# A spectral mix and a 32-head attention on one core: exponentials' buffers given out from a list of free ones

## The chip, the cores and the metric

The kernel runs on one core of one Trainium2 chip. The core has five engines that run side by side, each with an instruction queue of its own: TensorE (PE, matmuls; PEld is its weight loads), VectorE (DVE), ScalarE (ACT), GpSimd (POOL) and SyncE (SP), which here issues all DMAs. Engines wait for each other by semaphores: an instruction can wait until a counter of another engine, or of its own, has reached a value. The metric is the device time of one execution in microseconds (us), lower is better.

## The reference

Two branches work on the same x of 2048 tokens by 640 features and are mixed by a gate for each token. Branch A is a Fourier mix over tokens and features, of which the real part is kept. Branch B is attention with 32 heads of 20 features, one key and one value head for all of them.

```python
a = x @ Wd_re.T;  b = x @ Wd_im.T                  # 640 x 640, along the features
yA = Ws_re @ a - Ws_im @ b                         # 2048 x 2048, along the tokens
q = (x @ wq) as 32 heads of 20;  k = x @ wk;  v = x @ wv
p = softmax(q @ k.T * 20 ** -0.5)                  # per head, 2048 x 2048
yB = concat(p @ v) @ wo
g = sigmoid((x * gate_w).sum(-1))
out = g * yA + (1 - g) * yB
```

## The kernel before

The first part projects q, k and v and forms a and b of branch A. The long middle part, of which the change is a part, runs both branches interleaved. The last part multiplies by wo and mixes.

The middle part runs over 16 pairs of heads; p is the pair, hh the head in it. For each pair there are 16 rounds: two halves qh of the queries, and eight steps kk, each of two blocks of 128 keys. A round issues by a table, a string of words:

- **b** (`b_unit`, from line 728): one matmul of scores for 128 keys and 512 queries into a PSUM bank, then one exponential on ScalarE from that bank to an SBUF buffer `pt` of 128x512. Eight a round. The exponentials of a round are numbered 0 to 7 here, in the order of the table.
- **V** (`av_step`, from line 745): the four matmuls that multiply four `pt` buffers by the values, which appear as eight in the trace (a burst of av). Two a round, and they work on the round before, which waits in the list `old`.
- **a** (`a_half`): a matmul of scores for the next pair and a VectorE reduction for its row maxima. Eight a round while pairs are left.
- **y** (`halves.run`): matmuls of branch A, in two row groups of the array; y0 uses rows 0 to 63, y1 rows 64 to 127, beside a and b of the other head in the other row group.
- **E**: moving a finished block of branch A out of PSUM on ScalarE.

The words carry the row group and the PSUM bank: `b1S3` is scores of head 1 in bank S3. Three of five rounds use `ROUND_10`, with 20 y, and then two use `ROUND_9`, with 18; the last pair uses `ROUND_LAST`, in which there are 48 y and no a. The order on PE, ACT, DVE and POOL is the order of the code, and the framework adds the semaphore waits. Banks are few, so a b reuses a bank that an earlier exponential of the same round has read: in every half of a round, the last b of one row group goes to the bank of exponential 0 (first half) or 4 (second half), and its weight load waits for that exponential.

The `pt` buffers come from a pool of 16 under one name (line 524), so that the pool gives them out in turn: an exponential takes the buffer of the exponential 16 before it. Before it may write, three things must have happened: its own scores are there, the av matmul that read the old content is done, and the exponential that wrote the old content is done. The first two are counts of PE, the third is a count of ACT itself. An ACT instruction carries one wait; for a second the framework puts a separate wait instruction, EVENT_SEMAPHORE, ahead of it in the queue, unless it can tell that one wait implies the other. In the built program ScalarE has 1211 of these, and 937 of them belong to line 739, the exponentials.

Of the kernel before, what the change touches and what calls it, by code (L numbers as in the profile page):

```python
# [8 lines left out]
F32 = mybir.dt.float32  # L9
# [8 lines left out]
P = 128  # L18
# [5 lines left out]
NT = S // P  # L24
# [5 lines left out]
ROW = 512  # L30
# [3 lines left out]
def kernel(  # L34
# [24 lines left out]
    def bank(tag, name):  # L59
        if tag in BANKS:  # L60
            turn[tag] += 1
            tag = BANKS[tag][(turn[tag] - 1) % len(BANKS[tag])]
        return psum.tile([P, ROW], F32, tag=tag, name=name, bufs=1)
# [290 lines left out]
    def tick():  # L354
        clock["n"] += 1
        due = [t for t in todo if t[0] <= clock["n"]]
        todo[:] = [t for t in todo if t[0] > clock["n"]]
        for _, f, args in due:
            f(*args)
# [4 lines left out]
    def a_half(hh, tag="A", main=False):  # L364
        u = state[hh]
        if u >= NA:
            return
        ins = a_unit(u, hh, tag)
        if main:
            halves.scored(ins)  # L370
        state[hh] = u + 1
        if state[1 - hh] <= u:
            return
        if u % 64 == 16 and u // 64 + 1 < NPAIR:
            load_qs(u // 64 + 1)
        if u % 64 == 63:
            later(1, a_reduce, u // 64)
            later(3, a_final, u // 64)
# [142 lines left out]
    cp = ctx.enter_context(tc.tile_pool(name="cp", bufs=1))  # L521
    cpools += [cp, cp]
    xp = ctx.enter_context(tc.tile_pool(name="xp", bufs=1))
    pp = ctx.enter_context(tc.tile_pool(name="pp", bufs=16))
    op = ctx.enter_context(tc.tile_pool(name="op", bufs=2))


# [118 lines left out]
    def y_evict():  # L646

        if not ended:
            return
        grp = ended[0]  # L650
        ps = grp["ps"]
        if "t" not in grp:
            grp["t"] = [op.tile([P, HALF], F32, name=("yt", "yu")[k]) for k in range(len(ps))]
            grp["left"] = list(range(len(ps)))
        k = grp["left"].pop(0)
        nc.scalar.activation(grp["t"][k], ps[k], AF.Copy)  # L656
        if not grp["left"]:
            ended.pop(0)
            y_out(grp)
# [65 lines left out]
    av = {}  # L725
    pt = {}

    def b_unit(p, hh, kc, qc, tag="B"):
        b = 64 * hh
        ps = bank(tag, f"b_{p}_{kc}_{qc}_{hh}")  # L730
        nc.tensor.matmul(  # L731
            ps,
            ks[b : b + 62, kc * P : (kc + 1) * P],
            qs[p][b : b + 62, qc * ROW : (qc + 1) * ROW],
            start=True,
            stop=True,
        )
        t = pp.tile([P, ROW], F32, name="pt")
        halves.scored(nc.scalar.activation(t, ps, AF.Exp, scale=SCALE))  # L739
        pt[(hh, kc, qc)] = t  # L740

    def av_mm(ps, g, t, kc, first, last):
        nc.tensor.matmul(ps[32 * g : 32 * g + 32, :], vsb[:, kc, :], t, start=first, stop=last)  # L743

    def av_step(p, qh, kc):
        if kc == 0:
            av[qh] = bank("V", f"av_{p}_{qh}")
        for hh in range(2):
            for j in range(2):
                av_mm(av[qh], 2 * hh + j, pt.pop((hh, kc, 2 * qh + j)), kc, kc == 0, kc == NT - 1)  # L750

    def finish_half(p, qh):
        ob = op.tile([P, ROW], F32, name="ob")
        nc.scalar.activation(ob, av[qh], AF.Copy)
        for hh in range(2):
            h = 2 * p + hh
            for j in range(2):
                js = slice((2 * qh + j) * ROW, (2 * qh + j + 1) * ROW)
                g = 32 * (2 * hh + j)
                move(sum_d[h : h + 1, js], ob[g + DH : g + DH + 1])  # L760
                move(oT_d[h * DH : (h + 1) * DH, js], ob[g : g + DH])
        if p == LAST:
            sm = op.tile([P, 16], F32, name="sm")
            ts = slice(qh * S // 2, (qh + 1) * S // 2)
            for hh in range(2):
                move(sm[64 * hh : 64 * hh + 64], sum_d[2 * p + hh, ts].rearrange("(s t) -> s t", t=16))
            later(4, finish_last, ts, sm)
        elif qh == 1:
            sm = op.tile([P, 32], F32, name="sm")
            move(sm, sum_d[2 * p : 2 * p + 2].rearrange("h (s t) -> (h s) t", t=32))  # L770
            later(24, finish_sums, p, sm)
# [11 lines left out]
    def finish_last(ts, sm):  # L783
# [9 lines left out]

    ROUND_10 = (
        "a1S0 y0 b1S3 y0 y0 b1S1 y0 y0 a1S2 y0 a1S5 y0 y0 a1S4 y0 b1S0 b0S3 V a0S1 y1 y1 b0S0 "
        "y1 y1 a0S5 y1 a0S3 y1 y1 b0S2 y1 y1 a0S4 y1 b0S0 b1S1 V y0"
    ).split()
    ROUND_9 = (  # L800
        "a1S2 y0 b1S0 y0 y0 a1S1 y0 a1S5 y0 y0 a1S4 y0 y0 b1S3 y0 b0S2 b1S0 V a0S5 y1 b0S2 y1 "
        "y1 a0S1 y1 b0S0 y1 y1 a0S3 y1 y1 a0S4 y1 E0 b1S2 b0S5 V"
    ).split()

    ROUND_LAST = (
# [3 lines left out]
    ).split()  # L809
    ROUNDS = [(p, qh, kk) for p in range(NPAIR) for qh in range(2) for kk in range(NT // 2)]  # L810

# [7 lines left out]
    for rnd in ROUNDS:  # L819
        p, qh, kk = rnd  # L820
        nb, na = [0, 0], 0
        turn = (p * NT + qh * SJ + kk) % 5
        new = [(p, qh, 2 * kk), (p, qh, 2 * kk + 1)]
        for what in ROUND_LAST if p == LAST else ROUND_10 if turn < 3 else ROUND_9:
            if what == "V":
                if old:
                    st = old.pop(0)
                    av_step(*st)
                    if st[2] == NT - 1:
                        finish_half(*st[:2])  # L830
                continue
            g = int(what[1])
            if what[0] == "y":
                halves.run(g)
            elif what[0] == "E":
                if p == LAST or turn == 4:
                    y_evict()
            elif what[0] == "b":
                b_unit(p, g, 2 * kk + nb[g] // 2, 2 * qh + nb[g] % 2, what[2:])
                if p == LAST and sum(nb) % 2 == 0:  # L840
                    tick()
                nb[g] += 1
            else:
                if na % 2 == 0:
                    tick()
                a_half(g, what[2:], True)
                na += 1
        old += new
        if p == LAST and qh == 1:
            for f in BEFORE.get(kk, ()):  # L850
                f()
# [7 lines left out]
    for i in range(2 * NT):  # L859
        tb, e = divmod(i, 2)  # L860
        if e == 0:
            gate_y(tb + 1)
        o_group(tb, e)
        tick()
        if i == 0:
            for st in old:
                av_step(*st)
            finish_half(*old[-1][:2])
        n, k = divmod(i, 4)
        if k == 1:  # L870
            mult_o(n + 2)
        elif k == 2:
            split_o(n + 2)
            load_o(n + 3 if n else NO)
        if e == 1:
            load_y(tb + 4)
# [47 lines left out]
```

## Time and profile before

| what | value |
|---|---|
| median of 3 runs | 1837.29 us |
| the three runs | 1836.1, 1837.29 and 9650.36 us |
| the profiled execution's own time | 1837.41 us |
| its span, first to last instruction | 1835.6 us |
| granted TensorE clock | 1.0 throughout |
| exponentials (line 739) | 2048, mean 598 ns |

The profile is one execution, recorded by the hardware. The page gives each engine's busy time and its share of the span, the chain of work that ended last, and groups of instructions by source line. A group's row reads: line, engine, operation, output<-input, shapes, count, busy time and mean time of one, and then the engine's idle time ahead of these instructions with what ended it. In the timeline a row is: start, length, engine, line, operation, names, count of merged instructions, and the idle time before with its releaser. Ends of matmuls are modelled. Times of the timeline are rounded to 0.01 us.

The middle part runs from about 260 us to 1590 us in the ordinary rounds and to about 1765 us in the last pair's.

### The profile page before, as it was taken

To read this page: it belongs to the slowest core of one execution; us is meant where nothing else is said; L and a number is where in the kernel's file an instruction comes from. 1 tells how busy PE (TensorE), PEld (TensorE's weight loads), DVE (VectorE), ACT (ScalarE), POOL (GpSimd) and SP (SyncE) were. 2 spreads that over 40 slices of the span, in tenths; PEclk is the share of its full clock that TensorE was granted. 3 is DMA by queue.
4 is the path that set the end of the run, shared out by engine and by line. 5 is a ranking of instruction groups with operands and counts; after the bars stand their busy time and mean duration, and the time that the engine had idled before them with its cause. 6 is when DMAs were issued, how large, how long until landed. Compare 5 with 4: busy or idle time off the path is not lost.

```text
span 1835.6 us, 41674 instructions
## 1 busy us (share of the span) xinstructions
PE 1819.7 (99%) x16344; PEld 1231.3 (67%) x16344; DVE 1451.5 (79%) x2331; ACT 1238.6 (67%) x2327; POOL 817.1 (45%) x550
## 2 busy tenths in 40 slices
PE   8999999999999999999999999999999999999999
PEld 6799986666666666666666666666666666667789
DVE  4459998888888888888888888888888888853354
ACT  4322247777777777777777777777777777777731
POOL 0011227444455554556665555565554344342142
PEclk9999999999999999999999999999999999999999
DMA  7673324333434343534343434253433232324666
GB/s 248 182 227 105 113 98 143 100 116 84 136 90 150 105 138 99 157 121 147 115 150 117 154 107 147 94 155 108 152 110 113 78 120 85 97 65 151 213 213 211
DMA packets 131649, 243.94 MB, mean 133 GB/s; under 512 B 26356, under 2 KB 77556, under 8 KB 128932
## 3 DMA queue, kind: packets, MB, share of 16 engines
q1 hardware_dynamic: 131452, 241.27, 41.9%
q8 instruction: 128, 2.10, 0.5%
q14 instruction: 69, 0.57, 0.1%
HBM read 194.62 MB, written 50.86 MB: 134 GB/s over the span
## 4 chain that ended last, share of the span: by engine, by line
PE 95%; DMA 3%; SPq 1%; DVE 1%; ACT 1%; issue 0%; ACTq 0%; DVEq 0%
PE av L743 28%; PE y L630 20%; PE a L315 18%; PE b L731 16%; PE ab L124 7%; PE o L113 1%; PE o L114 1%; PE o L115 1%; SPq L105 1%; DMA ql_d<-ql 1%; DMA wraw<-in_wq_dram 1%; PE q L115 0%; PE q L113 0%; DMA wraw<-in_wiT_dram 0%; PE q L114 0%; DMA wraw<-in_wrT_dram 0%
## 5 line engine op out<-in xcount | busy, mean ns | idle before, releaser
L322 DVE TENSOR_REDUCE mx<-a 128x1 f32<-128x512 f32 x2048 | 1291.7, 684 | 188.2 <-PE a L315 179.4
L739 ACT ACTIVATE pt<-b 128x512 f32<-128x512 f32 x2048 | 1111.3, 598 | 356.0 <-PE b L731 303.4
L630 PE MATMUL y<-x,ch 64*128 64x320 f32 x3584 | 796.3, 317 | 2.2 <-ACT pt L739 1.1
L315 PE MATMUL a<-ks,qs 60*128 60x512 f32 x2048 | 739.5, 416 | 0.0
L630 PEld LDWEIGHTS y<-x,ch 64*128 64x128 f32 x3584 | 552.3, 184 | 87.2 <-ACT pt L739 83.7
L731 PE MATMUL b<-qs,ks 62*128 62x512 f32 x2048 | 606.7, 417 | 0.1
L315 PEld LDWEIGHTS a<-ks,qs 60*128 60x128 f32 x2048 | 379.6, 185 | 277.0 <-ACT pt L739 198.2
L743 PE MATMUL av<-pt,vsb 128*32 128x512 f32 x4096 | 542.0, 604 | 0.0
L630 PE MATMUL y<-x,cl 64*128 64x320 f32 x1792 | 528.3, 311 | 0.0
L731 PEld LDWEIGHTS b<-qs,ks 62*128 62x128 f32 x2048 | 323.4, 184 | 34.2 <-ACT pt L739 15.2
L630 PEld LDWEIGHTS y<-x,cl 64*128 64x128 f32 x1792 | 314.6, 184 | 41.1 <-ACT pt L739 41.1
L435 POOL TENSOR_TENSOR craw<-craw 128x1024 f32<-128x1024 f32 x80 | 191.1, 2388 | 234.2 <-DMA craw<-in_cre_dram 86.8
L440 POOL TENSOR_TENSOR cl<-craw,ch 128x1024 fp32r<-128x1024 f32 x98 | 234.2, 2389 | 7.9
L439 POOL CAST ch<-craw 128x1024 fp32r<-128x1024 f32 x98 | 101.7, 1038 | 196.2 <-PE y L630 159.3
L743 PEld LDWEIGHTS av<-pt,vsb 128*32 128x32 f32 x4096 | 82.3, 108 | 130.4 <-issue 122.6
L124 PE MATMUL ab<-wh,xh 64*128 64x320 f32 x640 | 133.7, 308 | 3.1 <-DVE both L510 1.9
L124 PE MATMUL ab<-wl,xh 64*128 64x320 f32 x640 | 133.2, 306 | 0.0
L124 PE MATMUL ab<-wh,xl 64*128 64x320 f32 x640 | 132.9, 305 | 0.0
L683 POOL TENSOR_TENSOR ya<-yt,ya 128x320 f32<-128x320 f32 x64 | 58.5, 931 | 147.5 <-ACT yt L656 146.9
L480 POOL TENSOR_TENSOR x<-both,x 128x320 fp32r<-128x320 f32 x16 | 19.2, 1202 | 217.7 <-ACT x L479 217.7
L509 ACT ACTIVATE half<-ab 128x320 f32<-128x320 f32 x64 | 28.0, 437 | 113.7 <-PE ab L124 109.8
L124 PEld LDWEIGHTS ab<-wh,xl 64*128 64x128 f32 x640 | 95.4, 184 | 0.0
(86 smaller groups left out, 1148.5 us busy)
## 6 DMA issues: line engine op xcount, KB each, us to landing
craw<-in_cre_dram SPq DMA_DIRECT2D x96, 512.0 KB
craw<-in_cim_dram SPq DMA_DIRECT2D x96, 512.0 KB
xr<-x_d SPq DMA_DIRECT2D x88, 320.0 KB
x_d<-both SPq DMA_DIRECT2D x64, 160.0 KB
qs<-qh_d SPq DMA_DIRECT2D x64, 160.0 KB
ya<-y_d SPq DMA_DIRECT2D x64, 160.0 KB
y_d<-ya SPq DMA_DIRECT2D x64, 160.0 KB
xr<-in_xT_dram SPq DMA_DIRECT2D x20, 256.0 KB
```

Of the source, the lines that this page charges most:

```text
L124: nc.tensor.matmul(ps, w[r], x[r], start=(i == 0 and k == 0), stop=(i == n - 1 and k == 2))
L315: nc.tensor.matmul(ps, qs[p][b : b + 60, qb * P : (qb + 1) * P], ks[b : b + 60, c * ROW : (c + 1) * ROW], start=True, stop=True,)
L322: return nc.vector.tensor_reduce(mx[p][:, hh, qb, c : c + 1], ps, axis=AX.X, op=ALU.max)
L435: eng.tensor_tensor(raw, raw, raws[1], op=PRODUCTS[n][0][1])
L439: eng.tensor_copy(h, raw)
L440: eng.tensor_tensor(l, raw, h.bitcast(F32), op=ALU.subtract)
L509: nc.scalar.activation(half, ps[0], AF.Copy, scale=sg)
L630: mm = nc.tensor.matmul(ps[g % len(ps)], w, x, start=start, stop=stop)
L683: nc.gpsimd.tensor_tensor(ya, yt, ya, op=how)
L731: nc.tensor.matmul(ps, ks[b : b + 62, kc * P : (kc + 1) * P], qs[p][b : b + 62, qc * ROW : (qc + 1) * ROW], start=True, stop=True,)
L739: halves.scored(nc.scalar.activation(t, ps, AF.Exp, scale=SCALE))
L743: nc.tensor.matmul(ps[32 * g : 32 * g + 32, :], vsb[:, kc, :], t, start=first, stop=last)
```

## The change

The pool gets one buffer under each of 16 names. A list, `ptfree`, holds the numbers of the free ones. A b takes a number from it, from the front (the one that has been free for the longest) or from the end (the one that was freed last), and av_step appends the numbers when it has issued the matmuls that read them. The table says which: words that begin with c instead of b take from the end. Where a word was b and is now c, row group and bank are as before.

```diff
-    pp = ctx.enter_context(tc.tile_pool(name="pp", bufs=16))
+    pp = ctx.enter_context(tc.tile_pool(name="pp", bufs=1))
...
-    def b_unit(p, hh, kc, qc, tag="B"):
+    ptfree = list(range(16))
+
+    def b_unit(p, hh, kc, qc, tag, newest):
...
-        t = pp.tile([P, ROW], F32, name="pt")
+        slot = ptfree.pop(-1 if newest else 0)
+        t = pp.tile([P, ROW], F32, tag=f"pt{slot}", name="pt")
         halves.scored(nc.scalar.activation(t, ps, AF.Exp, scale=SCALE))
-        pt[(hh, kc, qc)] = t
+        pt[(hh, kc, qc)] = t, slot
...
-                av_mm(av[qh], 2 * hh + j, pt.pop((hh, kc, 2 * qh + j)), kc, kc == 0, kc == NT - 1)
+                t, slot = pt.pop((hh, kc, 2 * qh + j))
+                av_mm(av[qh], 2 * hh + j, t, kc, kc == 0, kc == NT - 1)
+                ptfree.append(slot)
...
     ROUND_9 = (
-        "a1S2 y0 b1S0 y0 y0 a1S1 y0 a1S5 y0 y0 a1S4 y0 y0 b1S3 y0 b0S2 b1S0 V a0S5 y1 b0S2 y1 "
-        "y1 a0S1 y1 b0S0 y1 y1 a0S3 y1 y1 a0S4 y1 E0 b1S2 b0S5 V"
+        "a1S2 y0 b1S0 y0 y0 a1S1 y0 a1S5 y0 y0 a1S4 y0 y0 b1S3 y0 c0S2 c1S0 V a0S5 y1 b0S2 y1 "
+        "y1 a0S1 y1 c0S0 y1 y1 a0S3 y1 y1 a0S4 y1 E0 b1S2 c0S5 V"
     ).split()
...
-            elif what[0] == "b":
-                b_unit(p, g, 2 * kk + nb[g] // 2, 2 * qh + nb[g] % 2, what[2:])
+            elif what[0] in "bc":
+                b_unit(p, g, 2 * kk + nb[g] // 2, 2 * qh + nb[g] % 2, what[2:], what[0] == "c")
```

In ROUND_10 exponentials 1, 3, 6 and 7 become c, in ROUND_9 exponentials 2, 3, 5 and 7, in ROUND_LAST 1, 3, 5 and 7.

No instruction changes its place on any engine, and each exponential waits for the same count of PE. The second waits on ScalarE change. In the two places below, ScalarE's queue is shown as built; a row is line, operation, output<-input, size and the semaphores waited for. The input is named b, then block of keys, block of 512 queries, head and a running number; PE_49 counts matmuls, Activation_49 counts ScalarE's own instructions.

Before, ScalarE in the first ROUND_9 round of a cycle, the one that begins near 1003 us (pair 8):

```order
L739 ACTIVATE pt<-b_0_0_1_15688 128x512 [waits PE_49,Activation_49]
L739 ACTIVATE pt<-b_0_1_1_15717 128x512 [waits PE_49,Activation_49]
L739 ACTIVATE pt<-b_0_0_0_15722 128x512 [waits PE_49]
L739 ACTIVATE pt<-b_1_0_1_15726 128x512 [waits PE_49]
L739 ACTIVATE pt<-b_0_1_0_15738 128x512 [waits PE_49,Activation_49]
L739 ACTIVATE pt<-b_1_0_0_15748 128x512 [waits PE_49]
L739 ACTIVATE pt<-b_1_1_1_15763 128x512 [waits PE_49]
L739 ACTIVATE pt<-b_1_1_0_15767 128x512 [waits PE_49,Activation_49]
```

The same eight exponentials, 0 to 7, in the changed kernel:

```order
L744 ACTIVATE pt<-b_0_0_1_15688 128x512 [waits PE_49]
L744 ACTIVATE pt<-b_0_1_1_15717 128x512 [waits PE_49]
L744 ACTIVATE pt<-b_0_0_0_15722 128x512 [waits PE_49,Activation_49]
L744 ACTIVATE pt<-b_1_0_1_15726 128x512 [waits PE_49]
L744 ACTIVATE pt<-b_0_1_0_15738 128x512 [waits PE_49]
L744 ACTIVATE pt<-b_1_0_0_15748 128x512 [waits PE_49]
L744 ACTIVATE pt<-b_1_1_1_15763 128x512 [waits PE_49]
L744 ACTIVATE pt<-b_1_1_0_15767 128x512 [waits PE_49]
```

Exponentials 0, 1, 4 and 7 have lost the wait for ScalarE's own count, exponential 2 has gained one.

The second place is ScalarE in a ROUND_10 round that follows a ROUND_9 round, the one that begins near 1015 us; before:

```order
L739 ACTIVATE pt<-b_4_0_1_15891 128x512 [waits PE_49,Activation_49]
L739 ACTIVATE pt<-b_4_1_1_15897 128x512 [waits PE_49,Activation_49]
L739 ACTIVATE pt<-b_5_0_1_15916 128x512 [waits PE_49]
L739 ACTIVATE pt<-b_4_0_0_15920 128x512 [waits PE_49]
L739 ACTIVATE pt<-b_4_1_0_15933 128x512 [waits PE_49,Activation_49]
L739 ACTIVATE pt<-b_5_0_0_15948 128x512 [waits PE_49,Activation_49]
L739 ACTIVATE pt<-b_5_1_0_15958 128x512 [waits PE_49]
L739 ACTIVATE pt<-b_5_1_1_15962 128x512 [waits PE_49]
```

The same eight in the changed kernel:

```order
L744 ACTIVATE pt<-b_4_0_1_15891 128x512 [waits PE_49]
L744 ACTIVATE pt<-b_4_1_1_15897 128x512 [waits PE_49,Activation_49]
L744 ACTIVATE pt<-b_5_0_1_15916 128x512 [waits PE_49]
L744 ACTIVATE pt<-b_4_0_0_15920 128x512 [waits PE_49]
L744 ACTIVATE pt<-b_4_1_0_15933 128x512 [waits PE_49]
L744 ACTIVATE pt<-b_5_0_0_15948 128x512 [waits PE_49]
L744 ACTIVATE pt<-b_5_1_0_15958 128x512 [waits PE_49]
L744 ACTIVATE pt<-b_5_1_1_15962 128x512 [waits PE_49]
```

Exponentials 0, 4 and 5 have lost the second wait, exponential 1 keeps it. Over the whole program, 889 exponentials lose theirs, 112 gain one and 48 keep one; ScalarE's wait instructions go from 1211 to 434.

More of the change, by code (lines that the diff above doesn't have):

```diff
@@ L796 @@
     ROUND_10 = (
-        "a1S0 y0 b1S3 y0 y0 b1S1 y0 y0 a1S2 y0 a1S5 y0 y0 a1S4 y0 b1S0 b0S3 V a0S1 y1 y1 b0S0 "
-        "y1 y1 a0S5 y1 a0S3 y1 y1 b0S2 y1 y1 a0S4 y1 b0S0 b1S1 V y0"
+        "a1S0 y0 b1S3 y0 y0 c1S1 y0 y0 a1S2 y0 a1S5 y0 y0 a1S4 y0 b1S0 c0S3 V a0S1 y1 y1 b0S0 "
+        "y1 y1 a0S5 y1 a0S3 y1 y1 b0S2 y1 y1 a0S4 y1 c0S0 c1S1 V y0"
     ).split()
     ROUND_9 = (
-        "a1S2 y0 b1S0 y0 y0 a1S1 y0 a1S5 y0 y0 a1S4 y0 y0 b1S3 y0 b0S2 b1S0 V a0S5 y1 b0S2 y1 "
-        "y1 a0S1 y1 b0S0 y1 y1 a0S3 y1 y1 a0S4 y1 E0 b1S2 b0S5 V"
+        "a1S2 y0 b1S0 y0 y0 a1S1 y0 a1S5 y0 y0 a1S4 y0 y0 b1S3 y0 c0S2 c1S0 V a0S5 y1 b0S2 y1 "
+        "y1 a0S1 y1 c0S0 y1 y1 a0S3 y1 y1 a0S4 y1 E0 b1S2 c0S5 V"
     ).split()
     ROUND_LAST = (
[3 rows of a table removed]
[3 rows of a table added]
     ).split()
```

6 rows, old and new, of the table ROUND_LAST are left out of this document.

## The prediction, made before the changed kernel ran

> **What bounds the kernel now.** I read the page first, its busy times and the chain that ended last, then the exponentials' group, then the list of waits, then the timeline at the places where the change touches ScalarE.
>
> ```profile
> span 1835.6 us, 41674 instructions
> PE 1819.7 (99%) x16344; PEld 1231.3 (67%) x16344; DVE 1451.5 (79%) x2331; ACT 1238.6 (67%) x2327; POOL 817.1 (45%) x550
> PE 95%; DMA 3%; SPq 1%; DVE 1%; ACT 1%; issue 0%; ACTq 0%; DVEq 0%
> L739 ACT ACTIVATE pt<-b 128x512 f32<-128x512 f32 x2048 | 1111.3, 598 | 356.0 <-PE b L731 303.4
> ```
>
> TensorE looks full, 99% busy and 95% of the chain, and ScalarE looks slack, with 356 us of idle time before its exponentials. Taken at its word, this says that nothing done on ScalarE can matter. The list of waits and the source view of line 739 have one small row each that disagrees:
>
> ```profile
> PEld b L731 <- ACT pt L739: 15.2, 93, 0.3
> L739 ACTq EVENT_SEMAPHORE  x937: 17/17/17, 270.6 to 1753.0; - x188
> ```
>
> The first says that weight loads for scores (b) stood still 93 times until an exponential had ended. The second says that 937 separate wait instructions stand on ScalarE's queue beside the 2048 exponentials. In the stretch of five-round cycles, the windows view of av counts its work:
>
> ```profile
> 260.00:1590.00 1330.00, 485.44 (x3648) 71.76 (x3648) 16.98 (x28) 1.00 0.39 121
> ```
>
> The first count is TensorE's matmuls. A burst of av has 8, so 3648 / 8 = 456 bursts in 1330 us. I call the time from one burst to the next a half-round; half-rounds take about 2.91 us. Here is the second half of a ROUND_10 round, TensorE and ScalarE alone:
>
> ```profile
> 1045.37 0.16 PEld L743 LDWEIGHTS av<-pt,vsb 128*32 128x32 f32 x8 [0.24 <-issue]
> ...
> 1046.71 0.40 PE L731 MATMUL b<-qs,ks 62*128 62x512 f32 x1
> ...
> 1047.20 0.60 ACT L739 ACTIVATE pt<-b 128x512 f32<-128x512 f32 x1 [0.69 <-PE b L731]
> ...
> 1047.41 0.40 PE L731 MATMUL b<-qs,ks 62*128 62x512 f32 x1
> ...
> 1047.65 0.39 PE L315 MATMUL a<-ks,qs 60*128 60x512 f32 x1
> 1047.79 0.31 PE L630 MATMUL y<-x,ch 64*128 64x320 f32 x1
> 1047.85 0.19 PEld L731 LDWEIGHTS b<-qs,ks 62*128 62x128 f32 x2
> 1047.88 0.47 PE L731 MATMUL b<-qs,ks 62*128 62x512 f32 x2
> ...
> 1048.28 0.12 PEld L743 LDWEIGHTS av<-pt,vsb 128*32 128x32 f32 x3 [0.25 <-issue]
> ```
>
> The chain is: b ends at 1046.71 + 0.40 = 1047.11; its exponential starts 0.09 later, ends at 1047.80; the weight load of the next b in the same bank starts 0.05 later; the av burst follows 0.43 after that load. TensorE is shown busy throughout, but its last step before every av waits for ScalarE. The same 0.05 and 0.42 to 0.43 return in each half-round quoted below, so the pace is a ring through TensorE and ScalarE.
>
> **What a second wait costs.** The very first rounds have fresh buffers and therefore one wait per exponential. The same place of a ROUND_10 round there:
>
> ```profile
> 265.91 0.16 PEld L743 LDWEIGHTS av<-pt,vsb 128*32 128x32 f32 x8 [0.28 <-PE y L630]
> ...
> 267.25 0.40 PE L731 MATMUL b<-qs,ks 62*128 62x512 f32 x1
> ...
> 267.68 0.60 ACT L739 ACTIVATE pt<-b 128x512 f32<-128x512 f32 x1 [0.60 <-PE b L731]
> ...
> 268.33 0.19 PEld L731 LDWEIGHTS b<-qs,ks 62*128 62x128 f32 x2
> ...
> 268.42 0.45 PE L731 MATMUL b<-qs,ks 62*128 62x512 f32 x2
> 268.80 0.16 PEld L743 LDWEIGHTS av<-pt,vsb 128*32 128x32 f32 x8 [0.28 <-issue]
> ```
>
> b ends at 267.65 and the exponential starts 0.03 later, not 0.09: a wait instruction ahead of an exponential for which ScalarE is idle costs 0.06 us. The half-round took 268.80 - 265.91 = 2.89 us against 2.91 above. So of the 0.06 only 0.02 came through: the two last b then ended at 268.42 + 0.45 = 268.87, set by the stream of matmuls ahead of them, and av's load came 0.07 before that end.
>
> **The change part by part.** Matmuls, exponentials, DMAs and their order on all five engines stay as they are, and each exponential waits for the same TensorE count: nothing is moved past a queue, no byte is added, the 16 buffers take the same space, and DVE, POOL and SP keep their instructions and waits. These parts cost nothing because nothing in them differs. What goes is 777 of ScalarE's 1211 wait instructions: 889 exponentials lose their second wait, 112 gain one, 48 keep theirs. The earlier exponential that the second wait was for is 16 back, some 11 us at four in 2.91 us, so it never held anything up; its price is only the instruction.
>
> The losers include exponentials 0 and 4 of all five kinds of round, counted within a round, and those are the two that the last b of each half waits for. They run with ScalarE idle before them, so each should start 0.06 earlier. How much of it reaches av is set by the stream behind it, half by half. The second half of a ROUND_9 round:
>
> ```profile
> 1006.54 0.60 ACT L739 ACTIVATE pt<-b 128x512 f32<-128x512 f32 x1 [0.39 <-PE b L731]
> ...
> 1006.85 0.31 PE L630 MATMUL y<-x,ch 64*128 64x320 f32 x1
> 1006.99 0.39 PE L315 MATMUL a<-ks,qs 60*128 60x512 f32 x1
> 1006.99 0.31 PE L630 MATMUL y<-x,cl 64*128 64x320 f32 x1
> 1007.19 0.18 PEld L731 LDWEIGHTS b<-qs,ks 62*128 62x128 f32 x2 [0.16 <-ACT pt L739]
> ...
> 1007.62 0.16 PEld L743 LDWEIGHTS av<-pt,vsb 128*32 128x32 f32 x8 [0.25 <-issue]
> ```
>
> The exponential ends at 1007.14, the load follows at 1007.19. A y occupies its row group for about 0.14 (1006.85 to 1006.99), an a or b for about 0.24 (b at 1047.41, a at 1047.65, one row group), so without the wait the two b could run from 1007.13 and 1007.23 and take 0.39, the later ending at 1007.62; less 0.07, av at 1007.55. The cap is 0.07, so the whole 0.06 comes through. Three more halves:
>
> ```profile
> 1009.44 0.60 ACT L739 ACTIVATE pt<-b 128x512 f32<-128x512 f32 x1
> ...
> 1009.90 0.37 PEld L731 LDWEIGHTS b<-qs,ks 62*128 62x128 f32 x2
> ...
> 1010.52 0.16 PEld L743 LDWEIGHTS av<-pt,vsb 128*32 128x32 f32 x8 [0.25 <-PE b L731]
> ```
>
> ```profile
> 1015.25 0.60 ACT L739 ACTIVATE pt<-b 128x512 f32<-128x512 f32 x1 [0.51 <-PE b L731]
> ...
> 1015.70 0.38 PEld L731 LDWEIGHTS b<-qs,ks 62*128 62x128 f32 x2
> ...
> 1016.32 0.16 PEld L743 LDWEIGHTS av<-pt,vsb 128*32 128x32 f32 x8 [0.24 <-issue]
> ```
>
> ```profile
> 1003.64 0.60 ACT L739 ACTIVATE pt<-b 128x512 f32<-128x512 f32 x1 [0.63 <-PE b L731]
> ...
> 1004.23 0.24 PEld L731 LDWEIGHTS b<-qs,ks 62*128 62x128 f32 x2
> ...
> 1004.71 0.16 PEld L743 LDWEIGHTS av<-pt,vsb 128*32 128x32 f32 x8 [0.25 <-issue]
> ```
>
> The later of the two loads starts 0.18 before the row's end: 1010.09, 1015.90 and 1004.29, each 0.05 after its exponential's end and 0.42 to 0.43 ahead of av. Read in the same way, the first two (first half of a ROUND_9 round behind another, first half of a ROUND_10 round behind ROUND_9) have caps of 0.07 to 0.09, the third (first half of the first ROUND_9 round) 0.02. Of the ten halves of a five-round cycle four give 0.06, the two ROUND_9 second halves and the two just named, and six give 0.02: one cycle 4 x 0.06 + 6 x 0.02 = 0.36 us. With 456 half-rounds, 45.6 cycles: 16.4 us. Behind the gain the next limit is the stream itself in six halves, and still the exponential in four.
>
> The 112 new second waits stand behind a running exponential. The row nearest to that is a pair of which the second has two waits before the change:
>
> ```profile
> 1015.25 1.09 ACT L739 ACTIVATE pt<-b 128x512 f32<-128x512 f32 x2 [0.51 <-PE b L731]
> ```
>
> Two exponentials of 0.60 in 1.09: the second starts 0.49 after the first, so its wait is covered. I take 0 of the bounds 0 and 0.06. If the cover goes, 91 of them (2 of 10 half-rounds) delay a y, priced below. The last 16 rounds, with 48 y each, gain nothing in my sum; one exponential's 0.06 in each half would be 1.9 us either way.
>
> The sum is made against the profiled execution's own 1837.4 us (span 1835.6, 1.8 around it), 0.1 above the median of 1837.29: 1837.4 - 16.4 = 1821.
>
> [...]
>
> **The rivals.** *Hidden anyway*: the exponentials come earlier and the half-rounds stay at 2.91 because another wait, DVE's for a bank, ends as late. For it: DVE is 79% busy. Against it: the early half-round of 2.89. It gives 1837. [...]
>
> *The whole 0.06 everywhere*: the streams' caps are softer than read. 456 x 0.06 = 27.4, so 1810. Against it again: the early half-round shows 0.02.
>
> *Slower*: exponential 2 of ROUND_9 rounds now has two waits, and a y right behind av waits for it:
>
> ```profile
> 1005.06 1.08 ACT L739 ACTIVATE pt<-b 128x512 f32<-128x512 f32 x2
> ...
> 1005.71 0.18 PEld L630 LDWEIGHTS y<-x,ch 64*128 64x128 f32 x1
> ```
>
> It ends at 1005.06 + 0.60 = 1005.66, and y's load starts at 1005.71: no slack. If its new wait costs 0.06 and the gains stay away, 91 x 0.06 = 5.5 and 1843. It decides once ScalarE is idle ahead of this exponential; now it runs back to back.
>
> *Half of it*: the six stream-bound halves give nothing: 45.6 x 0.24 = 10.9, so 1826.5. That the waits do not go is excluded by the rows of the built program.
>
> **How the numbers follow.** Forecast 1821: 0.60. Half of it: 0.11. Hidden anyway: 0.13. The whole 0.06: 0.09. Slower: 0.04. 0.03 for what I have not seen. The range 1810 to 1829 takes in the forecast, half of it and the whole 0.06, 0.80 together; what is left out lies above, but for the unseen. 2% of 1837 is 37 us, about what a measurement here can tell from no change, and no case reaches it: faster by over 2% needs 0.08 us in every half-round, about the highest cap. Faster 0.02, within 2% 0.97, slower 0.01.
>
> **What would show it.** Right: about 160 wait instructions at the exponentials in place of 937; exponentials 0 and 4 of a round starting 0.03 behind b's end; ROUND_9 second halves near 2.85 and most ROUND_10 halves near 2.89; the row of b's loads waiting for exponentials well below 15.2. Wrong: half-rounds still 2.91 with a wait for DVE ahead of the last b, or y's load behind av later than before.

## The result, and the profile after

The changed kernel took 1817.96 us (median of 5 runs, 1816.94 to 1818.48), the kernel before 1837.29 beside it. Of the five runs of before one took 9650.36 us; without it the other four average 1836.62 and the changed kernel's five 1817.72, 18.9 us less, and the ratio is 0.9897, with a 95% interval of 0.9881 to 0.9913. That is 1.0% faster, a difference that is sure and lies inside the 2%. The prediction said 1821, between 1810 and 1829.

The page of the changed kernel, in the order in which the prediction read that of before: span, busy times, chain, the exponentials' group.

```profile
span 1815.1 us, 40897 instructions
PE 1801.7 (99%) x16344; PEld 1215.6 (67%) x16344; DVE 1455.0 (80%) x2331; ACT 1240.9 (68%) x2327; POOL 818.4 (45%) x550
PE 96%; DMA 2%; SPq 1%; DVE 1%; ACT 1%; issue 0%; ACTq 0%; DVEq 0%
L744 ACT ACTIVATE pt<-b 128x512 f32<-128x512 f32 x2048 | 1111.0, 597 | 334.8 <-PE b L735 297.7
```

Nothing on the page's first lines tells where 20.5 us of span went. TensorE is 99% busy as before, its weight loads 67% as before, and the mean exponential is as long. The small rows tell it. In the source view of line 744, the wait instructions at the exponentials:

```profile
L744 ACTq EVENT_SEMAPHORE  x160: 17/17/17, 275.9 to 1738.5; - x160
```

160 in place of 937. In the list of waits the row of b's weight loads standing still for exponentials, 15.2 us in 93 waits before, is gone; only these two rows of loads of b are left, and both were there before:

```profile
PEld b L735 <- issue: 6.7, 8, 0.8
PEld b L735 <- ACT yu L656: 6.7, 8, 0.8
```

That the row is gone does not mean that no load waits any more. The list takes idle times over 0.15 us alone. In the records of the trace before, 89 of the 93 lie in the second halves of the ROUND_9 rounds, with 0.16 in the median, and four are rare longer ones (below). In the changed kernel TensorE's weight loads still stand idle 0.10 us at the same place of those halves.

Here is the second half of a ROUND_10 round in the timeline, the same round that the prediction showed:

```profile
1033.00 0.16 PEld L748 LDWEIGHTS av<-pt,vsb 128*32 128x32 f32 x8 [0.25 <-issue]
...
1034.34 0.40 PE L735 MATMUL b<-qs,ks 62*128 62x512 f32 x1
1034.77 1.79 ACT L744 ACTIVATE pt<-b 128x512 f32<-128x512 f32 x3 [0.60 <-PE b L735]
...
1035.42 0.19 PEld L735 LDWEIGHTS b<-qs,ks 62*128 62x128 f32 x2
1035.52 0.45 PE L735 MATMUL b<-qs,ks 62*128 62x512 f32 x2
1035.89 0.16 PEld L748 LDWEIGHTS av<-pt,vsb 128*32 128x32 f32 x8 [0.28 <-issue]
```

b ends at 1034.74 and its exponential starts at 1034.77: 0.03 behind it, where it was 0.09. The half-round took 1035.89 - 1033.00 = 2.89 us. Exponential 4 ends about 1035.37 (0.60 each), the weight load follows, but av now comes 0.47 behind that load and not 0.43: the last b end at 1035.97, held by the stream of matmuls ahead of them. So a part of the 0.06 was lost here. The second half of the ROUND_9 round that the prediction showed:

```profile
992.95 0.16 PEld L748 LDWEIGHTS av<-pt,vsb 128*32 128x32 f32 x8 [0.28 <-issue]
...
994.28 0.40 PE L735 MATMUL b<-qs,ks 62*128 62x512 f32 x1
...
994.72 2.26 ACT L744 ACTIVATE pt<-b 128x512 f32<-128x512 f32 x4 [0.37 <-PE b L735]
...
995.37 0.19 PEld L735 LDWEIGHTS b<-qs,ks 62*128 62x128 f32 x2
...
995.80 0.16 PEld L748 LDWEIGHTS av<-pt,vsb 128*32 128x32 f32 x8 [0.25 <-issue]
```

995.80 - 992.95 = 2.85, where it was 2.91. The exponential ends at 994.72 + 0.60 = 995.32, the load comes 0.05 later and av 0.43 behind the load: this half still hangs on ScalarE, and nearly all of the 0.06 came through.

To see all ten halves of a five-round cycle at once I took, from the records of both traces, the time from the start of one burst of av to the next, and its median over the 47 or 48 cycles. (t,h) is half h (0 or 1) of round t of the cycle; t 0 to 2 are ROUND_10, 3 and 4 ROUND_9.

| half | (0,0) | (0,1) | (1,0) | (1,1) | (2,0) | (2,1) | (3,0) | (3,1) | (4,0) | (4,1) |
|---|---|---|---|---|---|---|---|---|---|---|
| before, ns | 2904 | 2909 | 2897 | 2914 | 2903 | 2909 | 2901 | 2907 | 2902 | 2907 |
| after, ns | 2838 | 2887 | 2883 | 2890 | 2879 | 2890 | 2883 | 2853 | 2839 | 2838 |
| gain, ns | 66 | 22 | 14 | 24 | 24 | 19 | 18 | 54 | 63 | 69 |

Together 373 ns a cycle; with 48 cycles 17.9 us. From the first exponential to the first of the last pair the trace before takes 1395.1 us and the trace after 1376.2: 18.9 less. Most of the difference of 1.0 lies in four halves (1,1) of before that a median does not show, each 0.27 us longer than the others. One of them:

```profile
877.85 0.40 PE L731 MATMUL b<-qs,ks 62*128 62x512 f32 x1
...
878.62 1.09 ACT L739 ACTIVATE pt<-b 128x512 f32<-128x512 f32 x2 [0.99 <-PE y L630]
...
879.27 0.18 PEld L731 LDWEIGHTS b<-qs,ks 62*128 62x128 f32 x2 [0.29 <-ACT pt L739]
```

b ends at 878.25 and exponential 4 starts 0.37 behind it, where 0.10 is usual in this trace. `t_oldest` below has such late gates at the same four places, `e_gate_two` at six; in the changed kernel no gate is later than 0.13. What delays them is not shown. The other 1.7 of the 20.5 us between the two spans lie ahead of the first exponential, at 259.7 and 258.1 us. The change does not reach there, and over all the traces of this document that start lies anywhere from 258.1 to 260.3.

### The profile page after: what moved, and what is told of

It reads as the page before. It is cut to its first block, busy times and chain, and to the rows that moved or that the text cites. A ratio compares the mean times of both kernels' runs of the same rounds, so it can differ in the third digit from the quotient of the medians.

```text
span 1815.1 us, 40897 instructions
## 1 busy us (share of the span) xinstructions
PE 1801.7 (99%) x16344; PEld 1215.6 (67%) x16344; DVE 1455.0 (80%) x2331; ACT 1240.9 (68%) x2327; POOL 818.4 (45%) x550
## 4 chain that ended last, share of the span: by engine, by line
PE 96%; DMA 2%; SPq 1%; DVE 1%; ACT 1%; issue 0%; ACTq 0%; DVEq 0%
PE av L748 28%; PE y L630 21%; PE a L315 18%; PE b L735 15%; PE ab L124 7%; PE o L113 1%; PE o L115 1%; PE o L114 1%; SPq L105 1%; DMA ql_d<-ql 1%; PE q L115 1%; PE q L113 1%; PE q L114 1%; DMA wraw<-in_wiT_dram 0%; DMA x_d<-both 0%; DMA wraw<-in_wq_dram 0%
## 5 line engine op out<-in xcount | busy, mean ns | idle before, releaser
L735 PE MATMUL b<-qs,ks 62*128 62x512 f32 x2048 | 596.5, 404 | 0.0
L735 PEld LDWEIGHTS b<-qs,ks 62*128 62x128 f32 x2048 | 314.5, 185 | 22.8 <-issue 6.7
```

Source lines behind the costliest of these rows:

```text
L735: nc.tensor.matmul(ps, ks[b : b + 62, kc * P : (kc + 1) * P], qs[p][b : b + 62, qc * ROW : (qc + 1) * ROW], start=True, stop=True,)
```

## The experiments

Theory: what the change saves is the separate wait instruction ahead of exponentials 0 and 4 of each round, the gates of the two half-rounds (a gate is an exponential for which the last loads of a half-round wait), and nothing else of it counts. Rivals: the list of buffers or their addresses matter, not the waits; or every wait instruction of the 777 removed has its share.

**The list without its effect, and other addresses.** In `t_oldest` every c of the three tables is a b again (one of the lines is shown), so that the buffers come out of the new list in the old turn.

```diff
-        "y1 y1 a0S5 y1 a0S3 y1 y1 b0S2 y1 y1 a0S4 y1 c0S0 c1S1 V y0"
+        "y1 y1 a0S5 y1 a0S3 y1 y1 b0S2 y1 y1 a0S4 y1 b0S0 b1S1 V y0"
```

> The changed kernel with its free list and its 16 names, but every word takes the buffer that has been free for the longest. ScalarE then has the 1211 wait instructions of the kernel before, 937 of them at the exponentials. Theory (the gain comes from exponentials 0 and 4 losing their second wait): 1836 to 1838 us, half-rounds of 2.90 to 2.91 us, the row of b's loads waiting for exponentials back near 15 us. Rival (the gain comes from the list or from where the buffers lie, not from the waits): 1817 to 1820 us.

Measured: 1835.67 us, ratio to before 1.0001 (0.9992 to 1.0009). The list of waits has the old row again, and the half-rounds are 2.90 to 2.91 in all ten places.

```profile
PEld b L735 <- ACT pt L744: 13.6, 83, 0.3
```

In `s_perm` the choice and the waits are those of the changed kernel, but each number names another buffer.

```diff
-        t = pp.tile([P, ROW], F32, tag=f"pt{slot}", name="pt")
+        t = pp.tile([P, ROW], F32, tag=f"pt{(5 * slot + 3) % 16}", name="pt")
```

> The changed kernel with the same list and the same 434 wait instructions, in which the number from the list is turned into another buffer (5 times the number, plus 3, modulo 16), so that every exponential writes to another address. Theory: 1817 to 1819 us. Rival (addresses of the buffers matter): another time by more than 2 us.

Measured: 1817.98 us, ratio 0.9902 (0.9888 to 0.9915), as the changed kernel. List and addresses are out as causes; the gain is in the waits.

**Which waits.** The next four kernels are the changed kernel with a second wait put back by hand: an exponential also waits for an earlier exponential. With `i` the number of the exponential in its round, `e_gate_two` does so at 0 and 4:

```diff
-        halves.scored(nc.scalar.activation(t, ps, AF.Exp, scale=SCALE))
+        ins = nc.scalar.activation(t, ps, AF.Exp, scale=SCALE)
+        if exps and (p != LAST and i in (0, 4)):
+            tc.add_manual_dep(ins.ins, exps[-1], ORDER, reason="a second wait")
+        exps.append(ins.ins.name)
+        halves.scored(ins)
```

> The changed kernel with its buffers, in which exponentials 0 and 4 of every round but the last pair's also wait for the exponential just before them on ScalarE, which is long done; all other exponentials have one wait or what they had. 769 wait instructions on ScalarE. Theory (two gates a round are all that counts): the gain goes, 1834.5 to 1838 us. Rival (what counts is how many wait instructions ScalarE has in all): 335 of the 777 that went are back, so 43% of the 19.3 us is lost, about 1826 us. Rival (where the buffers lie): 1818 us.

Measured: 1836.46 us, ratio 1.0001 (0.9992 to 1.001). Two gates a round take the whole gain away again, with 769 wait instructions against 1211. The row of waits agrees:

```profile
PEld b L737 <- ACT pt L746: 16.3, 99, 0.3
```

`e_rest_two` has the condition turned round: `i not in (0, 4)`.

> The reverse: exponentials 1, 2, 3, 5, 6 and 7 of every round but the last pair's wait for the exponential just before them as well, and exponentials 0 and 4 keep one wait. 1729 wait instructions on ScalarE, more than before the change. Theory (only 0 and 4 count, the others run behind a running exponential or have time): 1817 to 1821 us. Rival (the number of wait instructions counts): 1729 against 434 and 1211, by 19.3 us for 777 that is 32 us more, about 1850 us. Between the two: an exponential among the six that runs with ScalarE idle and holds up a matmul.

Measured: 1839.41 us, ratio 1.002 (1.0011 to 1.0029). The theory missed by some 20 us, and the reason is in my experiment. Two exponentials of one row of the timeline, here and, at the same place, in the next kernel, `e_rest_old`:

```profile
1014.29 1.22 ACT L746 ACTIVATE pt<-b 128x512 f32<-128x512 f32 x2
```

```profile
1002.60 1.08 ACT L746 ACTIVATE pt<-b 128x512 f32<-128x512 f32 x2
```

The first pair stands 1.22 - 0.60 = 0.62 apart, the second 0.48. Neighbouring exponentials overlap: the next one starts about 0.10 before the recorded end of the one ahead. An exponential that waits for the one just before it, still running, loses this overlap; the wait that I had put in was a real one, and not just an instruction. ScalarE then gets late itself, and matmuls that wait for exponentials 2, 3 and 7 stand still. In the ROUND_9 second halves, (3,1) and (4,1), exponential 2 ends 1.16 and 1.15 us behind av in place of 0.91 and 0.95, and y's first load waits for it. Such a half in the timeline:

```profile
1005.18 0.16 PEld L754 LDWEIGHTS av<-pt,vsb 128*32 128x32 f32 x8 [0.32 <-issue]
...
1006.39 0.18 PEld L630 LDWEIGHTS y<-x,ch 64*128 64x128 f32 x1
...
1007.02 0.18 PEld L737 LDWEIGHTS b<-qs,ks 62*128 62x128 f32 x1
...
1008.19 0.16 PEld L754 LDWEIGHTS av<-pt,vsb 128*32 128x32 f32 x8 [0.28 <-issue]
```

In the records exponential 2 ends at 1006.34 and exponential 3 at 1006.97; y's load and the load of the b that goes to the bank of exponential 3 each come 0.05 behind. These two halves take 3.01 and 2.99 us. (1,0), (2,0) and (3,0) are longer too, 2.91 to 2.92: exponential 7 of the round before ends 1.50 behind av in place of 1.16, and the load of the next matmul for its bank comes at 1.56 in place of 1.34. The other five are as in the changed kernel.

`e_rest_old` mends that: the wait is for the exponential four before (`exps[-4]`).

> As e_rest_two, but the extra wait is for the exponential four before, which is long done, in place of the one just before, which still runs: behind a running exponential the spacing was 0.49 us with a wait that was met, and 0.63 us in e_rest_two. The program keeps the extra wait at 1, 2, 3, 5 and 7 where it isn't implied, never at 0, 4 or 6; 1056 wait instructions on ScalarE, 622 of the 777 are back. Theory (only exponentials 0 and 4 count, and what e_rest_two lost was the broken overlap): 1817 to 1821 us. Rival (the number of wait instructions counts): 80% of 19.3 us, 1833 us. Rival (exponential 1 of ROUND_9 and 2 and 5 of ROUND_10, which run with ScalarE idle, each hold up a matmul): some 1823 to 1828 us.

Measured: 1818.27 us, ratio 0.9907 (0.9893 to 0.992): no loss, with 782 wait instructions at exponentials in place of 160.

```profile
L746 ACTq EVENT_SEMAPHORE  x782: 17/17/17, 261.6 to 1739.8; - x196
```

This includes exponential 5 of ROUND_10, which runs with ScalarE idle and starts 0.096 behind its b in place of 0.036. It pays the 0.06, and the half-rounds stay within 8 ns of those of the changed kernel (the table below). Of these waits only those at the gates count.

**The two sizes.** `e_four_two` has the second wait back at the gates of the four halves that the prediction gave 0.06, `e_six_two` at those of the other six.

```diff
-        if exps and (p != LAST and i in (0, 4)):
+        if exps and (p != LAST and (turn, i) in ((0, 0), (3, 4), (4, 0), (4, 4))):
```

> The changed kernel, in which the second wait (for the exponential just before, done) is back at the gates of four of ten half-rounds alone, those that the forecast gave 0.06 us each: exponential 0 of the first ROUND_10 round and of the second ROUND_9 round, exponential 4 of both ROUND_9 rounds. Theory, with the half-rounds' medians of the two traces (66, 54, 63 and 69 ns longer before): 0.25 us a cycle, 48 cycles: 12 us more than after, 1829 to 1831 us, and these four halves alone return to 2.90. Rival (a half-round that is held up is made up for in the next): under 1824 us.

Measured: 1829.41 us, ratio 0.9964 (0.9951 to 0.9976), 11.4 above the changed kernel.

```diff
-        if exps and (p != LAST and i in (0, 4)):
+        if exps and (p != LAST and (turn, i) in ((0, 4), (1, 0), (1, 4), (2, 0), (2, 4), (3, 0))):
```

> The second wait is back at the gates of the other six of ten half-rounds alone, those that the forecast gave 0.02 us each. Theory, with the medians of the two traces (14 to 24 ns longer before, 0.12 us a cycle): 5.8 us more than after, 1823 to 1825 us. Rival (each gate costs the same 0.04 us, wherever it is): 11.6 us more, 1829.5 us. Rival (the streams hide it): 1818 us.

Measured: 1824.53 us, ratio 0.9936 (0.9923 to 0.9948), 6.6 above. The two together make 18.0, nearly the whole gain of 18.9, and each changes its own halves alone (the table below). Six gates that save 0.06 each give little more than half of what four give.

**What it is in a second wait that costs.** The prediction put the price on the instruction. In the built program of the kernel before, all 937 wait instructions at exponentials carry the wait for TensorE, which is met last, and the exponential behind it carries the wait for ScalarE, long met. Two kernels take this apart. `d_three4` adds to `e_gate_two` a wait for a VectorE reduction four before. The program gives the wait instruction VectorE's wait beside TensorE's.

```diff
             tc.add_manual_dep(ins.ins, exps[-1], ORDER, reason="a second wait")
+            tc.add_manual_dep(ins.ins, reds[-4], ORDER, reason="a third wait")
```

> As e_gate_two, but exponentials 0 and 4 also wait for a VectorE reduction four before, long done: three waits at seven of ten gates, two at the others, with the same 769 wait instructions as in e_gate_two, so one wait instruction carries two waits. Theory (the price is the instruction in the queue): as e_gate_two, 1835 to 1838 us. Rival (the price is the wait, 0.06 us each): seven gates of ten pay 0.06 more, 0.42 us a cycle, 48 cycles: about 1856 us.

Measured: 1833.24 us, ratio 0.9986 (0.9976 to 0.9995). A third wait costs nothing; the rival of 0.06 for each wait is out. The time is 2 us below the range that I gave. At the gates with three waits the exponential starts 0.086 behind b, with two 0.097, with one 0.037. Why three are 0.01 cheaper than two stays open, and so does why (1,0) and (2,0), with two, take 2.91 here (the table below).

`d_dve4` has the wait for the reduction alone, in place of that for an exponential.

```diff
-            tc.add_manual_dep(ins.ins, exps[-1], ORDER, reason="a second wait")
+            tc.add_manual_dep(ins.ins, reds[-4], ORDER, reason="a second wait")
```

> In the kernel before, all 937 wait instructions at the exponentials carry the wait for TensorE, the one that comes last, and the exponential itself carries the wait for ScalarE, long met. Here exponentials 0 and 4 of all but the last pair's rounds wait for a VectorE reduction four before in place of an exponential; the program keeps that second wait at seven of the ten gates, and there the wait instruction carries VectorE's, long met, and the exponential TensorE's. 765 wait instructions on ScalarE, four fewer than in e_gate_two. Theory (the price is paid only where the late wait is the one that stands in the separate instruction): 1817 to 1820 us, exponential 0.03 us behind b. Rival (any wait instruction ahead of an exponential for which ScalarE is idle costs 0.06): the seven halves return to their length before the change, 22 + 24 + 19 + 18 + 54 + 63 + 69 ns a cycle, 48 cycles, about 1831 us.

Measured: 1818.49 us, ratio 0.9904 (0.9891 to 0.9918). The ROUND_9 second half shown above, in the timeline of this kernel:

```profile
995.12 0.16 PEld L756 LDWEIGHTS av<-pt,vsb 128*32 128x32 f32 x8 [0.28 <-issue]
...
996.45 0.40 PE L739 MATMUL b<-qs,ks 62*128 62x512 f32 x1
...
996.89 1.79 ACT L748 ACTIVATE pt<-b 128x512 f32<-128x512 f32 x3 [0.38 <-PE b L739]
...
997.97 0.16 PEld L756 LDWEIGHTS av<-pt,vsb 128*32 128x32 f32 x8 [0.24 <-issue]
```

and in that of `e_gate_two`:

```profile
1003.28 0.16 PEld L754 LDWEIGHTS av<-pt,vsb 128*32 128x32 f32 x8 [0.25 <-issue]
...
1004.62 0.40 PE L737 MATMUL b<-qs,ks 62*128 62x512 f32 x1
...
1005.11 1.78 ACT L746 ACTIVATE pt<-b 128x512 f32<-128x512 f32 x3 [0.47 <-PE b L737]
1005.76 0.19 PEld L737 LDWEIGHTS b<-qs,ks 62*128 62x128 f32 x2 [0.16 <-ACT pt L746]
...
1006.19 0.16 PEld L754 LDWEIGHTS av<-pt,vsb 128*32 128x32 f32 x8 [0.24 <-issue]
```

Both have a wait instruction ahead of exponential 4. Here it starts 0.04 behind b's end (996.85) and the half-round takes 2.85 us; there 0.09 behind (1005.02) and 2.91. The wait instructions at exponentials number 491 here, 495 there.

So an instruction ahead in the queue costs nothing when its wait is met early. The 0.06 is paid when the wait that comes last stands in the separate instruction. One rival is left by these two kernels: wherever an exponential paid, it also waited for ScalarE's own count, and in `d_dve4` the gates do not. Another group of ScalarE's instructions speaks against it. The moves of branch A out of PSUM (E) carry, from about 800 us on, a wait for GpSimd, with TensorE's in a separate instruction: in the trace after, 28 of them start 0.05 to 0.06 ahead of the recorded end of the instruction before, where 18 earlier ones with one wait start 0.11 ahead. That is 0.06 without any wait for ScalarE. The copies of line 509, in the first part of the trace before, agree with the two kernels but leave the rival open: they start, in the median, 0.037 behind their matmul with one wait, 0.038 with VectorE's wait in the separate instruction and TensorE's on themselves, and 0.096 with TensorE's in the separate instruction and ScalarE's on themselves.

Why it is so no run of this case shows; measured are the 0.06 itself and the kernels that pay it.

**A faster one, tried.** Three ROUND_9 halves and (0,0) still hang on the exponential. `n_swap9` issues the b of the gates one word earlier in ROUND_9, `n_swap9_10` also in ROUND_10's first half.

```diff
-        "a1S2 y0 b1S0 y0 y0 a1S1 ... V a0S5 y1 b0S2 y1 "
+        "b1S0 y0 a1S2 y0 y0 a1S1 ... V b0S2 y1 a0S5 y1 "
```

> The changed kernel, in which ROUND_9 issues the b that feeds exponential 0 and the one that feeds exponential 4 one word earlier: b1S0 before a1S2, and b0S2 before a0S5. In the changed kernel the halves (3,1), (4,0) and (4,1) still end 0.42 us after the load that waits for these exponentials, 20 to 35 ns above what the matmuls ahead of it would allow. Theory: three halves of ten gain 0.02 to 0.035 each, 48 cycles, 3 to 5 us less: 1813 to 1815 us. Rival (the reductions of the a that come later hold a bank longer, or b in the first place waits for its bank): no gain or slower, 1818 to 1826 us.

```diff
-        "a1S0 y0 b1S3 y0 y0 c1S1 ..."
+        "b1S3 y0 a1S0 y0 y0 c1S1 ..."
```

> As n_swap9, and in ROUND_10 b1S3 also comes before a1S0, for the fourth half that the exponential still bounds, (0,0). Theory: another 0.02 to 0.03 us a cycle, about 1 us less than n_swap9. Rival: (1,0) and (2,0), which the matmuls bound, get longer by what b's weight load waits for behind av, and it is no faster than n_swap9.

Measured: 1833.7 us (ratio 0.9987, 0.9978 to 0.9996) and 1844.48 us (1.0043, 1.003 to 1.0055): 16 and 27 us slower than the changed kernel. The first lies past even its rival's 1826; the second is "no faster than `n_swap9`", as its rival said. A ROUND_9 second half of `n_swap9` in the timeline, from one av to the next, with VectorE's first reduction in it:

```profile
914.68 0.16 PEld L748 LDWEIGHTS av<-pt,vsb 128*32 128x32 f32 x8 [0.24 <-PE y L630]
...
916.21 1.92 ACT L744 ACTIVATE pt<-b 128x512 f32<-128x512 f32 x3 [0.19 <-PE b L735]
...
916.45 0.69 DVE L322 TENSOR_REDUCE mx<-a 128x1 f32<-128x512 f32 x1 [0.45 <-PE a L315]
...
916.96 0.41 PEld L735 LDWEIGHTS b<-qs,ks 62*128 62x128 f32 x2
917.10 0.58 PE L735 MATMUL b<-qs,ks 62*128 62x512 f32 x2
917.62 0.16 PEld L748 LDWEIGHTS av<-pt,vsb 128*32 128x32 f32 x8 [0.24 <-issue]
```

The exponential ends at 916.81, and the load that waits for it comes only at 916.96, 0.15 later: the exponential does not hold it. But the last b of the other row group goes to bank S5, which the first a of the half has used. VectorE's reduction of that a ends at 916.45 + 0.69 = 917.14, and the load starts 0.05 behind it, at 916.96 + 0.41 - 0.18 = 917.19; av follows 0.43 later. Now the same half in the changed kernel:

```profile
906.89 0.16 PEld L748 LDWEIGHTS av<-pt,vsb 128*32 128x32 f32 x8 [0.28 <-PE y L630]
...
908.42 1.29 DVE L322 TENSOR_REDUCE mx<-a 128x1 f32<-128x512 f32 x2 [0.40 <-PE a L315]
...
909.31 0.19 PEld L735 LDWEIGHTS b<-qs,ks 62*128 62x128 f32 x2
909.74 0.16 PEld L748 LDWEIGHTS av<-pt,vsb 128*32 128x32 f32 x8 [0.25 <-issue]
```

The reduction starts 908.42 - 906.89 = 1.53 behind av; in `n_swap9` 916.45 - 914.68 = 1.77, 0.24 later, because its a is issued later. With 0.69 for one it ended at 909.11, 0.20 ahead of the loads. The exponential that still holds its load ended 0.05 ahead of it. So the reduction is a second gate, which opens 0.15 before the first. The swap took the exponential out of the way and made the reduction later, and the half went from 2.85 to 2.93. In all four ROUND_9 halves one of the last two loads starts 0.05 behind a reduction, and so it does in the three ROUND_10 first halves of `n_swap9_10`, 2.94 us each. The first rival had named this place, with a price that was too low. No version here is faster than the changed kernel.

Half-rounds of the experiments, ns, in the manner of the table above:

| half | (0,0) | (0,1) | (1,0) | (1,1) | (2,0) | (2,1) | (3,0) | (3,1) | (4,0) | (4,1) |
|---|---|---|---|---|---|---|---|---|---|---|
| e_gate_two | 2904 | 2909 | 2899 | 2908 | 2899 | 2907 | 2904 | 2906 | 2900 | 2904 |
| e_rest_two | 2841 | 2887 | 2911 | 2884 | 2917 | 2884 | 2917 | 3009 | 2843 | 2992 |
| e_rest_old | 2846 | 2887 | 2883 | 2895 | 2878 | 2890 | 2883 | 2851 | 2841 | 2842 |
| e_four_two | 2906 | 2885 | 2883 | 2895 | 2879 | 2895 | 2879 | 2913 | 2912 | 2907 |
| e_six_two | 2832 | 2909 | 2899 | 2910 | 2900 | 2908 | 2902 | 2854 | 2841 | 2841 |
| d_dve4 | 2838 | 2889 | 2883 | 2890 | 2879 | 2890 | 2883 | 2853 | 2838 | 2838 |
| d_three4 | 2898 | 2895 | 2911 | 2895 | 2911 | 2895 | 2900 | 2895 | 2889 | 2891 |
| n_swap9 | 2838 | 2888 | 2883 | 2890 | 2879 | 2890 | 2944 | 2934 | 2937 | 2934 |
| n_swap9_10 | 2935 | 2890 | 2944 | 2884 | 2945 | 2884 | 2948 | 2934 | 2935 | 2933 |

`e_four_two` and `e_six_two` lengthen just the halves named for them, by 60 to 73 ns and by 16 to 22, and leave the others within 6 ns of the changed kernel.

## Why the prediction was right, point by point

**The ring.** Right. Two gates a round carry the whole effect: put back at 0 and 4 alone the second waits bring 1836.5, put back elsewhere 1818.3. That a TensorE at 99% and a ScalarE at 67% are in one ring could be read from the two small rows and the 0.05 and 0.43 in the halves. One half did not fit: the early one, with one wait, has 0.47 from the load (268.33) to av (268.80). The prediction's sentence that 0.42 to 0.43 return in each half passes over that; its next part uses it rightly, as the mark of a half that the matmuls bound.

**The price of 0.06.** Right in size: exponentials 0 and 4 start 0.036 behind b where they started 0.097. The step that said what is paid for was not right: "its price is only the instruction". `d_dve4` has the instruction at seven of ten gates and pays nothing. What costs is that the late wait stands in it. For this change both readings gave the same number, since all 937 wait instructions carried the late wait: that the wrong reading did no harm to the forecast was luck.

**The sum.** 16.4 was forecast; the medians give 17.9 and the traces' middle part 18.9. The four halves named for 0.06 gave 66, 54, 63 and 69 ns, together 252 where 240 was said; the six for 0.02 gave 14 to 24, together 121 where 120 was said. The larger part of the 1.5 up to 17.9 is the count. I took 456 half-rounds from a window that ends at 1590 us; the windows view of before shows av going on at that pace behind it:

```profile
1590.00:1655.00 65.00, 23.82 (x180) 3.46 (x176) 0.60 (x1) 1.00 0.23 71
```

180 / 8 are 22 more half-rounds until the last pair begins; 48 cycles in place of 45.6 make 17.3 of the same terms. The remaining 1.0 has no term in the sum: it is mostly the four late gates of before shown above, of which none is left after the change. The prediction did not have them.

**The caps.** Right: the rival with the whole 0.06 everywhere (1810) fails on the six halves, the rival in which those six give nothing (1826.5) on `e_six_two`, 6.6 us. "Hidden anyway" (1837) fails on both, since all ten halves got shorter.

**The new second waits.** Right to cost them at nothing: exponential 2 of ROUND_9 starts 0.494 behind exponential 1, with its new wait, as 0.493 before the change without one. The slower rival did not come. `e_rest_two` shows what it would have needed, a wait for an exponential still running, and there the y that this rival named does wait for exponential 2.

**The last 16 rounds.** Right: from their first exponential to the end of their last 105.2 us before and after.

**The busy shares.** Weight loads stayed at 67% and matmuls at 99% while the span fell by 20.5 us. Not taking the 99% at its word was right; how much there was to gain, neither share told.

## What to carry to other kernels

In a kernel with an engine at 99%, look for the short wait that ends last in each turn of the loop, even if the list of waits shows little of it. Here a row of 15 us in 1836 held two halves of ten and four rare waits, and the change was worth 18 to 19 us, from all ten: a list of idle times is not the price. Ahead of an instruction on such a gate, see that one wait is enough, or that the wait which comes last is the one that the instruction itself carries; a second wait for something long done was then free here. Before moving a gate forward, look for the next one behind it: here it was 0.15 us away, on another engine.

## What was not expected of the hardware

A separate wait instruction ahead of an exponential costs 0.06 us if it holds the wait that comes last (0.097 behind b in place of 0.037), and nothing if that one is held by the exponential itself (0.037 in `d_dve4`), with ScalarE idle in both cases.

Neighbouring exponentials of 0.60 us overlap by 0.10 (0.104 in the median of the pairs that overlap, before and after alike); a wait for the one just ahead brings the spacing from 0.49 to 0.63 (`e_rest_two`).

The 331 wait instructions with two waits in `d_three4` are recorded otherwise than those with one. In the source view the shortest, median and longest record in ns:

```profile
L748 ACTq EVENT_SEMAPHORE  x495: 17/1634/1663, 259.9 to 1754.7; - x165
```

The 164 with one wait stand with 17 ns, the 331 with two with 623 to 1663 ns. Two waits alone do not make the record long: 141 others on ScalarE in this trace have two and stand with 38 ns. What the long records hold no run shows.
